# A fused attention and MLP kernel: a new order of its first stage, earlier fetches, masks built in one step, and another warm-up

## The chip, the cores and the metric

The kernel runs on one core of a Trainium2 chip. The core has engines that work side by side, each with its own queue of instructions taken in order: TensorE (PE: matmuls, and transposes done as matmuls), VectorE (DVE), ScalarE (ACT), GpSimd (POOL) and SyncE (SP, which here only issues DMAs). Inputs lie in the chip's main memory and come by DMA into on-chip memory (SBUF); TensorE writes its results into eight banks of PSUM. The metric is the device time of one execution in microseconds, shorter is better. Before the change three runs took 713.47, 714.91 and 716.59 us.

## The reference

Attention with four sink keys and a sliding window of 128 keys, over 4 batches, 8 heads, 768 positions and 64 dimensions; its output is the input of a two-layer MLP (512 to 2048 to 512) with a leaky ReLU.

```python
scores = scale * np.matmul(q, k.transpose(0, 1, 3, 2))
...
is_sink = pos[None, :] < int(n_sink)
rel = pos[:, None] - pos[None, :]
in_window = (rel >= 0) & (rel < int(window))
keep = is_sink | in_window
scores = np.where(keep, scores, -1000000000.0)
scores = scores - np.max(scores, axis=-1, keepdims=True)
a = np.exp(scores)
a = a / (np.sum(a, axis=-1, keepdims=True) + 1e-09)
attn_out = np.matmul(a, v)
x = attn_out.transpose(0, 2, 1, 3).reshape(B * S, H * D)
h = x @ w_in
g = np.maximum(0.01 * h, h)
out = (g @ w_out).astype(np.float32)
```

The two limits, sinks and window, are inputs, so the masks are made on the chip. The weights arrive as 64-bit numbers and are turned into 32-bit ones on the chip ("decoded").

## The kernel before

**Units.** The positions are cut into `NU` = 8 units of 384 rows (half a batch), a unit into `T` = 3 tiles of 128 queries. For each unit and head a tile's queries meet only the keys of their window: two blocks of 128 keys with the four sink keys between them (`W3` = 260 columns), or one block (128 columns) for the very first tile.

**Two forms of attention.** Units 0 and 1 (`EARLY` = 2) work on pairs of heads with plain 32-bit matmuls. Their tile goes through these steps: `scores_pair` (two score matmuls, one for each head, L283); `softmax_pair` (on DVE one instruction per head adds the mask and takes the row's extreme, L303; on ACT one exponential per head, which also sums its row, L305); `tail_pair`, called a turn below (two or four transposes on PE, L354 and L355, and a copy of them to SBUF on ACT, L357 or L360; POOL copies the sink columns, L358). After the third tile of a pair come `sinks` (one transpose, L386, a DVE product, L390, and a POOL copy of the sums, L395) and `values_pair` (value matmuls L412 and L414, three transposes L418, a copy on ACT, L419, the product on DVE, L421, and `emit_x`, which splits the result into a rounded part and the rest, L515 on ACT and L516 on DVE). Units 2 to 7 work head by head with rounded operands (fp32r) and are not touched.

**The MLP.** A unit's 384 rows go through 16 blocks of 128 hidden columns: twelve matmuls into bank `h` (L559), the leaky ReLU on ACT and DVE (L566, L567), a rounded part and the rest (L568, L569), and nine matmuls into three output banks (L580). Bank `h` is single: the next block may start when L567 has read the last one.

**Weights.** `load_weights` fetches one block of 512 KB, decodes it in three DVE steps (L172, L174, L176), rounds it on ACT (L180) and takes the rest on POOL (L181). `pace` ties the fetch to a softmax that lies `PRED` steps back in the stream, or, once four are decoded, to the decode of the fourth last.

**Order.** PE's order is written out by hand: two streams of steps (attention and MLP) are drawn in turn, and PE runs them as drawn. The other engines' orders are set by a scheduler that places each instruction among them. First the attention stream alone takes `early_steps + LEAD0` = 32 + 5 steps, which is unit 0 and part of unit 1 (called the first stage here). In it the softmax and scores of tile j are drawn, then what is pending: up to three steps, among them the turn of the tile before. Then the MLP of unit 0 begins, with the attention of unit 1 laced into it; from then on each unit's MLP runs beside a later unit's attention. SP issues its DMAs in order too: one that waits for a free buffer holds up those behind it.

**Start.** While the first loads run, PE does `WARM` = 22 matmuls on a tile of zeros (L604). `build_masks` makes three masks on DVE (first tile, m1, m2) from distances that POOL counts (L79, L81) and from the limits (L71 to L102); POOL then spreads m1 and m2 to the 260 columns that the early form needs (`wide`, L137 and L139).

Of the kernel before, what the change touches and what calls it, by code (L numbers as in the profile page):

```python
# [9 lines left out]
F32 = mybir.dt.float32  # L10
# [34 lines left out]
LEAD0 = 5  # L45
# [9 lines left out]
WARM = 22  # L55
DEPTH = 4
PRE0 = 5
PRED = 7
# [5 lines left out]
def build_masks(nc, cpool, tpool, lims):  # L64
    raw = tpool.tile([P, 2, 2], I32, name="lim_raw")
    words = lims.bitcast(I32).rearrange("(o w) -> o w", o=1)
    nc.sync.dma_start(out=raw.rearrange("p i w -> p (i w)"), in_=words.broadcast_to([P, 4]))
    lo = tpool.tile([P, 2], F32, name="lim_lo")
    hi = tpool.tile([P, 2], F32, name="lim_hi")
    lim = cpool.tile([P, 2], F32, name="lim")  # L70
    nc.vector.tensor_copy(out=lo, in_=raw[:, :, 0])  # L71
# [4 lines left out]

    rel = tpool.tile([P, 2 * P], F32, name="rel")
    key = tpool.tile([P, P], F32, name="key")
    nc.gpsimd.iota(rel, pattern=[[-1, 2 * P]], base=P, channel_multiplier=1,  # L79
                   allow_small_or_imprecise_dtypes=True)  # L80
    nc.gpsimd.iota(key, pattern=[[1, P]], base=0, channel_multiplier=0,  # L81
                   allow_small_or_imprecise_dtypes=True)
    cur = tpool.tile([P, P], F32, name="cur")
    prv = tpool.tile([P, P], F32, name="prv")
    m0 = cpool.tile([P, P], F32, name="m0")
    m1 = cpool.tile([P, WM], F32, name="m1")
    m2 = cpool.tile([P, WM], F32, name="m2")
    tri = cpool.tile([P, P], I8, name="tri")
    nc.vector.tensor_scalar(out=cur, in0=rel[:, P:], scalar1=0.0, scalar2=None, op0=ALU.is_ge)
    nc.vector.tensor_scalar(out=tri, in0=rel[:, P:], scalar1=0.0, scalar2=None, op0=ALU.is_lt)  # L90
    nc.vector.scalar_tensor_tensor(out=cur, in0=rel[:, P:], scalar=win, in1=cur, op0=ALU.is_lt, op1=ALU.mult)
    nc.vector.scalar_tensor_tensor(out=m0, in0=key, scalar=ns, in1=cur, op0=ALU.is_lt, op1=ALU.max)
    nc.vector.tensor_scalar(out=m0, in0=m0, scalar1=-1.0, scalar2=MASKED, op0=ALU.add, op1=ALU.mult)
    nc.vector.tensor_scalar(out=prv, in0=rel[:, 0:P], scalar1=win, scalar2=None, op0=ALU.is_lt)
# [13 lines left out]
    return lim, (m0, m1, m2), tri, diag  # L108
# [3 lines left out]
def fast_path(ctx, tc, cpool, qp, qk, vu, vs, w_in, w_out, out, ident, wz, lim, masks, tri, diag, negm, wmin, wmax):  # L112
# [20 lines left out]
    wide = []  # L133
    for n, m in enumerate(masks[1:]):
        e = apool.tile([P, W3], F32, tag="stg", name=f"wide{n}")
        for sign, base, dst in ((1, -1, e[:, 0:P]), (-1, 0, e[:, WM:])):
            nc.gpsimd.affine_select(out=dst, in_=m[:, NSK:], pattern=[[sign, P]], base=base,  # L137
                                    channel_multiplier=-sign, compare_op=ALU.is_ge, fill=-MASKED)
        nc.gpsimd.tensor_copy(out=e[:, P:WM], in_=m[:, 0:NSK])  # L139
        wide.append(e)  # L140
# [310 lines left out]
    def attend_pair(u, pair, pend, state):  # L451
# [12 lines left out]
        def gather():  # L464
            state["st"] = sinks(u, pair, sk, state)
# [361 lines left out]
```

## Time and profile before

| | before |
|---|---|
| runs shown, median (lowest to highest) | 714.91 us (713.47 to 716.59) |
| profiled execution: its time | 712.43 us |
| its span in the trace | 710.7 us |
| mean granted TensorE clock | 0.995 |
| bytes moved, share of DMA busy (queue 1) | 74.32 MB, 32.0% |

The table stands for the profiled execution except for its first row. The span runs from the first to the last instruction in the trace; 1.7 us lie around it. A row of the timeline has its start and its length in us, the engine (PEld is the loading of PE's stationary operand, SPq an issue of a DMA), the line, the operation and what it writes and reads, the shapes and a count where equal instructions follow one another; in brackets stands how long the engine had been idle, and what ended that. A row of the windows gives for a stretch of time its length and, for each engine, the time that it was busy.

### The profile page before, as it was taken

The numbers are of one execution on the slowest core, as the hardware profiler recorded it, in microseconds if no ns is written. First come the engines' busy times: TensorE is split into PE (matmuls) and PEld (weight loads), VectorE is DVE, ScalarE is ACT, GpSimd is POOL, SyncE is SP. The second block draws the span as 40 slices with busy tenths as digits, with TensorE's granted clock in tenths as the row PEclk, the third lists the DMA queues.
The fourth block names the chain that finished last, engine by engine and source line by source line (L and its number), as shares of the span: only waits on it lengthen the run. The fifth ranks groups of instructions, "written<-read, shape, count | busy, mean of one in ns | idle before, by whom it ended". The sixth has DMA issues, their size and how long they took to land.

```text
span 710.7 us, 12473 instructions
## 1 busy us (share of the span) xinstructions
PE 692.1 (97%) x3871; PEld 602.9 (85%) x3871; DVE 533.9 (75%) x1717; ACT 417.8 (59%) x1162; POOL 397.4 (56%) x536
## 2 busy tenths in 40 slices
PE   8799999999999999999999999999999999999995
PEld 4467778999899899998989799989899998999884
DVE  6788989666678888888889888888888978642222
ACT  5766666576656666666665676666667566422221
POOL 2346668555557777667666777748666665400000
PEclk9999999999999999999999999999999999999999
DMA  6756654221124342243324433334332310000001
GB/s 189 262 171 227 204 170 167 67 74 56 54 70 139 125 127 92 96 155 117 101 97 132 127 123 108 99 106 144 103 100 98 102 54 30 0 19 28 1 0 50
DMA packets 42603, 74.32 MB, mean 105 GB/s; under 512 B 3489, under 2 KB 26273, under 8 KB 42529
## 3 DMA queue, kind: packets, MB, share of 16 engines
q1 hardware_dynamic: 42384, 73.31, 32.0%
q8 instruction: 33, 0.54, 0.3%
q14 instruction: 42, 0.34, 0.2%
q10 hardware_dynamic: 144, 0.13, 0.1%
HBM read 67.14 MB, written 6.29 MB: 103 GB/s over the span
## 4 chain that ended last, share of the span: by engine, by line
PE 89%; DVE 5%; ACT 2%; DMA 1%; issue 1%; POOL 1%; POOLq 0%; ACTq 0%; DVEq 0%
PE h L559 36%; PE o L580 36%; PE v L439 5%; PE s L291 4%; PE t L365 2%; PE v L412 1%; PE s L283 1%; DMA wiraw<-in_w_in 1%; PE v L414 1%; DVE gl L569 1%; DMA woraw<-in_w_out 1%; PE t L386 0%; PE t L433 0%; PE t L355 0%; PE t L418 0%
## 5 line engine op out<-in xcount | busy, mean ns | idle before, releaser
L559 PE MATMUL h<-xh,wi 128*128 128x384 f32 x1024 | 311.3, 352 | 1.7 <-DVE g L567 1.3
L580 PE MATMUL o<-wo,gh 128*128 128x512 f32 x768 | 247.1, 403 | 0.0
L559 PEld LDWEIGHTS h<-xh,wi 128*128 128x128 f32 x1024 | 190.0, 188 | 16.7 <-issue 2.5
L559 PE MATMUL h<-xl,wi 128*128 128x384 f32 x512 | 172.8, 337 | 0.0
L335 POOL TENSOR_SCALAR_AFFINE_SELECT pt<-stg 128x256 fp32r<-128x256 f32 x240 | 105.3, 463 | 95.1 <-DVE stg L373 71.5
L580 PE MATMUL o<-wo,gl 128*128 128x512 f32 x384 | 151.4, 394 | 0.0
L580 PEld LDWEIGHTS o<-wo,gh 128*128 128x128 f32 x768 | 132.3, 189 | 17.2 <-issue 0.7
L567 DVE TENSOR_TENSOR g<-h,g 128x384 f32<-128x384 f32 x128 | 71.0, 555 | 64.0 <-ACT g L566 63.0
L566 ACT ACTIVATE g<-h 128x384 f32<-128x384 f32 x128 | 62.4, 487 | 70.1 <-PE h L559 68.8
L559 PEld LDWEIGHTS h<-xl,wi 128*128 128x128 f32 x512 | 96.9, 189 | 3.0
L580 PEld LDWEIGHTS o<-wo,gl 128*128 128x128 f32 x384 | 72.1, 188 | 17.9 <-DVE gl L569 0.2
L568 ACT CAST gh<-g 128x384 fp32r<-128x384 f32 x128 | 65.5, 511 | 35.1 <-DVE g L567 32.6
L569 DVE TENSOR_TENSOR gl<-g,gh 128x384 fp32r<-128x384 f32 x112 | 76.4, 682 | 11.5 <-ACT gh L568 9.9
L320 ACT ACTIVATE pk<-pk,negm 128x128 f32<-128x128 f32 (+1 forms) x144 | 58.1, 404 | 37.8 <-DVE negm L317 37.2
L242 POOL TENSOR_TENSOR qksp<-qkraw,qksp 64x392 fp32r<-64x392 f32 (+1 forms) x48 | 58.5, 1219 | 25.9 <-ACT qksp L241 18.0
L291 PEld LDWEIGHTS s<-qksp 128*128 128x128 f32 x288 | 53.2, 188 | 9.3 <-issue 2.9
L372 ACT CAST stg<-t 128x128 fp32r<-128x128 f32 x120 | 31.0, 258 | 47.9 <-PE t L365 34.0
L291 PE MATMUL s<-qksp 128*128 128x260 f32 (+1 forms) x288 | 56.3, 277 | 2.4 <-DVE negm L317 2.4
L244 POOL TENSOR_TENSOR qksp<-qkraw,qksp 128x384 fp32r<-128x384 f32 x48 | 51.9, 1082 | 3.8
L326 DVE TENSOR_SCALAR pk<-pk,sm 128x132 f32<-128x132 f32 (+1 forms) x120 | 47.5, 396 | 2.1
L439 PEld LDWEIGHTS v<-pt,vsp 128*128 128x128 f32 x336 | 45.1, 189 | 2.7 <-DVE xf L445 0.6
L241 ACT CAST qksp<-qkraw 128x776 fp32r<-128x776 f32 (+1 forms) x48 | 42.9, 893 | 6.7 <-PE s L291 3.4
(132 smaller groups left out, 1058.8 us busy)
## 6 DMA issues: line engine op xcount, KB each, us to landing
qkraw<-in_qk SPq DMA_DIRECT2D x24, 454.0 KB, 3.3
qkraw<-in_qk SPq DMA_DIRECT2D x24, 388.0 KB, 3.6
wiraw<-in_w_in SPq DMA_DIRECT2D x16, 512.0 KB, 3.8
woraw<-in_w_out SPq DMA_DIRECT2D x16, 512.0 KB, 3.8
ciraw<-in_w_in SPq DMA_DIRECT2D x16, 512.0 KB, 3.7
coraw<-in_w_out SPq DMA_DIRECT2D x16, 512.0 KB, 3.5
out<-ob SPq DMA_DIRECT2D x23, 256.0 KB, 2.0
vraw<-in_vu SPq DMA_DIRECT2D x14, 256.0 KB, 2.6
```

The lines of the kernel that those rows point to most:

```text
L242: nc.gpsimd.tensor_tensor(out=sp[D:P, TU:TU + n], in0=raw[D:P, TU:TU + n], in1=sp[D:P, TU:TU + n].bitcast(F32), op=ALU.subtract)
L244: nc.gpsimd.tensor_tensor(out=sp[:, TU + n:2 * TU + n], in0=raw[:, 0:TU], in1=sp[:, 0:TU].bitcast(F32), op=ALU.subtract)
L291: nc.tensor.matmul(ps[:, 0:kn], lhsT=sp[:, off + j * P:off + (j + 1) * P], rhs=sp[:, TU + k0:TU + k0 + kn], start=c == 0, stop=c == len(pa ...
L320: nc.scalar.activation(out=w, in_=w, func=AF.Exp, scale=-1.0, bias=neg, accum_out=sm)
L335: nc.gpsimd.affine_select(out=out, in_=src, pattern=([[0, x]] if x > 1 else []) + [[sign, P]], base=-1 if prev else 0, channel_multiplier= ...
L439: nc.tensor.matmul(out[:, o:o + m], lhsT=l, rhs=r, start=c == 0, stop=c == len(mms) - 1, skip_group_check=True)
L559: nc.tensor.matmul(ph[:, 0:TU], lhsT=w[:, cs], rhs=x, start=cc == 0 and c == 0, stop=cc == NCC - 1 and c == 2)
L566: nc.scalar.mul(g, ph[:, 0:TU], 0.01)
L567: anchor[0] = nc.vector.tensor_tensor(out=g, in0=ph[:, 0:TU], in1=g, op=ALU.max)
L568: nc.scalar.copy(out=gh, in_=g)
L569: (nc.gpsimd if u == 0 else nc.vector).tensor_tensor(out=gl, in0=g, in1=gh.bitcast(F32), op=ALU.subtract)
L580: nc.tensor.matmul(po[t], lhsT=gg[:, tsl], rhs=w, start=f == 0 and c == 0, stop=f == NFC - 1 and c == 2)
```

## The change

- **Order of units 0 and 1.** `attend_pair` goes; `early_stream` runs over all 24 tiles in one loop. A tile's scores and softmax are drawn `SAHEAD` = 2 tiles ahead of its turn. After the third turn of a pair the sinks are drawn at once, and the values after the scores of the next tile.
- **Fetches.** The values of pair 1 are loaded at the start, those of later pairs two ahead. A weight fetch is tied to a softmax 12 steps back (`PRED`; 7 before), while the distance between two weight loads stays 7 (`PERIOD`) and the first comes one step later (`PRE0` 6, was 5).
- **First stage.** It ends two steps sooner (`LEAD0` 3, was 5); the MLP of unit 0 begins there, and the two steps follow inside it.
- **Masks.** `build_masks` makes the two wide masks on DVE straight from the distances. The narrow ones are folded from them later (`fold_masks`). The setting of `diag` goes from DVE to POOL, and three checks of the limits go to the end (`check_limits`).
- **Warm-up.** 12 matmuls on the zeros as before, then 4 on a rounded tile of zeros (`st1`).
- **Last output tile.** Its two halves lie in two tiles instead of one.

```diff
-LEAD0 = 5
+LEAD0 = 3
+SAHEAD = 2
-WARM = 22
+WARM = 12
+WARMR = 4
-PRE0 = 5
-PRED = 7
+PRE0 = 6
+PERIOD = 7
+PRED = 12
...
+    nc.vector.scalar_tensor_tensor(out=keep, in0=rel, scalar=win, in1=keep, op0=ALU.is_lt, op1=ALU.mult)
+    nc.vector.scalar_tensor_tensor(out=m0, in0=key, scalar=ns, in1=keep[:, WM:], op0=ALU.is_lt, op1=ALU.max)
     nc.vector.tensor_scalar(out=m0, in0=m0, scalar1=-1.0, scalar2=MASKED, op0=ALU.add, op1=ALU.mult)
...
+    nc.vector.tensor_scalar(out=wide[0], in0=keep, scalar1=-1.0, scalar2=MASKED, op0=ALU.add, op1=ALU.mult)
+    nc.vector.tensor_scalar(out=keep[:, P:WM], in0=key[:, 0:NSK], scalar1=ns, scalar2=None, op0=ALU.is_lt)
+    nc.vector.tensor_scalar(out=wide[1], in0=keep, scalar1=-1.0, scalar2=MASKED, op0=ALU.add, op1=ALU.mult)
...
+def fold_masks(nc, cpool, wide):
+    folded = [cpool.tile([P, WM], F32, name=f"m{n + 1}") for n in range(2)]
+    nc.vector.tensor_tensor(out=folded[0][:, NSK:], in0=wide[1][:, 0:P], in1=wide[1][:, WM:], op=ALU.max)
+    nc.gpsimd.tensor_copy(out=folded[1][:, NSK:], in_=folded[0][:, NSK:])
+    for e, m in zip(wide, folded):
+        nc.gpsimd.tensor_copy(out=m[:, 0:NSK], in_=e[:, P:WM])
+    return folded
...
-        pace(dma, decoded[-DEPTH] if len(decoded) >= DEPTH else anchors[-PRED])
+        pace(dma, decoded[-DEPTH] if len(decoded) >= DEPTH else anchors[-min(PRED, len(anchors))])
...
+        for k, tile_ in enumerate(tiles):
+            score(*tile_)
+            yield
+            while pend:
                 pend.pop(0)[1]()
                 yield
...
+            if k >= SAHEAD:
+                u, pair, j = tiles[k - SAHEAD]
+                turn(u, pair, j)
+                yield
+                if j == T - 1:
+                    gather(u, pair)
+                    yield
+                    pend.append((1, lambda u=u, pair=pair: value(u, pair)))
...
+                            nc.scalar.copy(out=obs[0], in_=po[t][:, 0:256])
+                            nc.scalar.dma_start(out=out[r0:r0 + P, 0:256], in_=obs[0])
+                            nc.vector.tensor_copy(out=obs[1], in_=po[t][:, 256:])
+                            nc.sync.dma_start(out=out[r0:r0 + P, 256:], in_=obs[1])
...
+    for _ in range(WARMR):
+        nc.tensor.matmul(warm[:, 0:TU], lhsT=sts[1][:, 0:P], rhs=sts[1], start=True, stop=True)
```

Three places show what this does to the engines' orders. In the names `s0_4_2` are the scores of unit 0, head 4, tile 2; `t` a transpose's bank, `pe0_2_1` the exponentials of unit 0, pair 2, tile 1; the last number only tells buffers apart.

PE before, from the scores of unit 0's pair 2 (heads 4 and 5), tile 2, to that tile's turn:

```order
L283 MATMUL s0_4_2_406<-qkp0_2_192 128x260
L283 MATMUL s0_5_2_407<-qkp0_2_192 128x260
L354 MATMUL t12_416<-ident_60,pe0_2_1_353 128x128
L355 MATMUL t12_416<-ident_60,pe0_2_1_353 128x128
L354 MATMUL t12_416<-ident_60,pe0_2_1_353 128x128
L355 MATMUL t12_416<-ident_60,pe0_2_1_353 128x128
L283 MATMUL s0_6_0_429<-qkn0_3_241 128x128
L283 MATMUL s0_7_0_430<-qkn0_3_241 128x128
L354 MATMUL t13_437<-ident_60,pe0_2_2_405 128x128
L355 MATMUL t13_437<-ident_60,pe0_2_2_405 128x128
```

PE of the changed kernel, first what follows the same scores, then where the same tile's turn stands:

```order
L284 MATMUL s0_4_2_340<-qkp0_2_167 128x260
L284 MATMUL s0_5_2_341<-qkp0_2_167 128x260
L413 MATMUL v0_1_350<-pt0_1_209,vn0_1_163 64x256 x4
L413 MATMUL v0_1_350<-pt0_1_209,vn0_1_163 64x128 x2
L415 MATMUL v0_1_350<-sn0_1_335,vsraw0_1_164 128x256
L419 MATMUL t10_358<-ident_60,rs1_337 128x128 x3
L356 MATMUL t11_373<-ident_60,pe0_2_0_291 128x128 x2
```

```order
L284 MATMUL s0_6_1_409<-qkn0_3_205 128x260
L284 MATMUL s0_7_1_410<-qkn0_3_205 128x260
L355 MATMUL t13_417<-ident_60,pe0_2_2_339 128x128
L356 MATMUL t13_417<-ident_60,pe0_2_2_339 128x128
L355 MATMUL t13_417<-ident_60,pe0_2_2_339 128x128
L356 MATMUL t13_417<-ident_60,pe0_2_2_339 128x128
L387 MATMUL t14_424<-ident_60,sk0_2_288 16x128
```

Between a tile's scores and its turn stood one turn and one pair of scores; now the values of a pair, a short turn (pair 2, tile 0), the scores of tile 0 of pair 3, the turn of tile 1 and the scores of tile 1 of pair 3 stand there.

DVE before, from the limits to the first softmax:

```order
L91 SCALAR_TENSOR_TENSOR cur_84<-rel_80,lim_75,cur_84 128x128
L94 TENSOR_SCALAR prv_85<-rel_80,lim_75 128x128
L99 TENSOR_SCALAR m2_88<-key_81,lim_75 128x4
L631 TENSOR_SCALAR bad_8872<-lim_75 128x1
L632 TENSOR_SCALAR bad_8872<-lim_75 128x1
L633 TENSOR_SCALAR bad_8872<-lim_75 128x1
L92 SCALAR_TENSOR_TENSOR m0_86<-key_81,lim_75,cur_84 128x128
L95 TENSOR_TENSOR m1_87<-cur_84,prv_85 128x128
L96 SCALAR_TENSOR_TENSOR m1_87<-key_81,lim_75,prv_85 128x4
L101 TENSOR_SCALAR m2_88<-m2_88 128x4
L93 TENSOR_SCALAR m0_86<-m0_86 128x128
L98 TENSOR_SCALAR m1_87<-m1_87 128x132
```

(then the two casts of `st` and a copy, L130 and L102). DVE of the changed kernel, the same stretch whole, with the first softmax:

```order
L93 SCALAR_TENSOR_TENSOR keep_111<-rel_109,lim_108,keep_111 128x260
L94 SCALAR_TENSOR_TENSOR m0_115<-key_110,lim_108,keep_111 128x128
L96 SCALAR_TENSOR_TENSOR keep_111<-key_110,lim_108,keep_111 128x4
L95 TENSOR_SCALAR m0_115<-m0_115 128x128
L98 TENSOR_SCALAR wide0_117<-keep_111 128x260
L99 TENSOR_SCALAR keep_111<-key_110,lim_108 128x4
L100 TENSOR_SCALAR wide1_118<-keep_111 128x260
L111 TENSOR_TENSOR m1_565<-wide1_118 128x128
L304 ISA pe0_0_0_172,negm_65<-s0_0_0_173,m0_115 128x128
```

Fifteen instructions behind the limits become eight; the casts of `st` now stand ahead of the limits, and the fold of the narrow mask (L111) was drawn up to just before the first softmax.

SP before, from its sixth DMA:

```order
L204 DMA qkp0_2_192<-in_qp0 128x776
L223 DMA vn0_1_219<-in_vu0 128x384
L223 DMA vsraw0_1_220<-in_vs 128x128
L204 DMA qkn0_3_241<-in_qp0 128x776
L152 DMA wiraw0_315<-in_w_in 128x4x256
L223 DMA vraw0_2_300<-in_vu0 128x384
L223 DMA vsraw0_2_301<-in_vs 128x128
L204 DMA qkn1_0_332<-in_qp1 128x908
L153 DMA woraw0_391<-in_w_out 128x1024
```

SP of the changed kernel, from the same place:

```order
L224 DMA vn0_1_163<-in_vu0 128x384
L224 DMA vsraw0_1_164<-in_vs 128x128
L205 DMA qkp0_2_167<-in_qp0 128x776
L153 DMA wiraw0_300<-in_w_in 128x4x256
L205 DMA qkn0_3_205<-in_qp0 128x776
L154 DMA woraw0_377<-in_w_out 128x1024
L205 DMA qkn1_0_286<-in_qp1 128x908
L224 DMA vraw0_2_278<-in_vu0 128x384
L224 DMA vsraw0_2_279<-in_vs 128x128
```

The first two weight blocks move ahead of loads that wait for buffers: `wiraw0` ahead of the queries and keys of pair 3, `woraw0` ahead of those of unit 1's first pair and of the values of pair 2.

More of the change, by code (lines that the diff above doesn't have):

```diff
@@ L75, in build_masks @@
     ns, win = lim[:, 0:1], lim[:, 1:2]
[L77 to L85, printed above, removed]
@@ L107, in build_masks, with fast_path @@
                                 channel_multiplier=sign, compare_op=ALU.is_ge, fill=0.0)
-    return lim, (m0, m1, m2), tri, diag
+    return lim, m0, wide, tri, diag
+def fold_masks(nc, cpool, wide):
[5 more added lines that the diff above has]
+    return folded
 @with_exitstack
-def fast_path(ctx, tc, cpool, qp, qk, vu, vs, w_in, w_out, out, ident, wz, lim, masks, tri, diag, negm, wmin, wmax):
+def fast_path(ctx, tc, cpool, qp, qk, vu, vs, w_in, w_out, out, ident, wz, lims, negm, wmin, wmax):
     nc = tc.nc
@@ L131, in fast_path @@
         sts.append(st)
[L133 to L140, printed above, removed]
+    lim, m0, wide, tri, diag = build_masks(nc, cpool, mpool, iopool, apool, lims)
+    masks = [m0]
     xs = [[] for _ in range(NU)]
@@ L482, in attend_late @@
+        pend.append((0, lambda: gather(u, pair)))
+        pend.append((1, lambda: value(u, pair)))
     def attend_late(u, h, pend, state):
@@ L526, in attention_stream @@
         load_values(0, 0)
-        for u in range(EARLY):
-            for pair in range(NPAIR):
-                yield from attend_pair(u, pair, pend, state[pair % 2])
+        load_values(0, 1)
+        yield from early_stream(pend)
         for u in range(EARLY, NU):
@@ L624, in fast_path, with check_limits @@
             next(stream, None)
-    return flags[0]
-def needs_general(nc, pool, row, ident, lim, negm, wmin, wmax):
+    return flags[0], lim
+def check_limits(nc, pool, lim):
     bad = pool.tile([P, 6], F32, name="bad")
-    deep = pool.tile([P, 1], F32, name="deep")
     nc.vector.tensor_scalar(out=bad[:, 0:1], in0=lim[:, 0:1], scalar1=float(NSK), scalar2=None, op0=ALU.is_gt)
@@ L633, in needs_general @@
     nc.vector.tensor_scalar(out=bad[:, 2:3], in0=lim[:, 1:2], scalar1=float(P), scalar2=None, op0=ALU.is_gt)
+    return bad
+def needs_general(nc, pool, row, ident, bad, negm, wmin, wmax):
+    deep = pool.tile([P, 1], F32, name="deep")
     nc.vector.tensor_reduce(out=deep, in_=negm, axis=AX.X, op=ALU.max)
```

115 lines of the change are left out of this document (58 added, 57 removed).

## The prediction

> **What bounds the kernel now.** I read the busy times first, then the slices, then windows, then TensorE's own waits.
>
> ```profile
> PE 692.1 (97%) x3871; PEld 602.9 (85%) x3871; DVE 533.9 (75%) x1717; ACT 417.8 (59%) x1162; POOL 397.4 (56%) x536
> ...
> PE   8799999999999999999999999999999999999995
> ...
> PE s L291 <- DVE negm L317: 2.4, 2, 1.5
> PE h L559 <- DVE g L567: 1.3, 1, 1.3
> ...
> 6.30:41.20 34.90, 28.76 (x181) 15.87 (x181) 25.00 (x94) 24.78 (x81) 9.79 (x24) 0.95 0.65 211
> 60.00:80.00 20.00, 20.00 (x115) 15.51 (x114) 18.09 (x40) 11.91 (x30) 11.66 (x13) 1.00 0.60 200
> ```
>
> TensorE is the bound: 97% busy, and in the 40 slices only the first three and the last fall short. The waits are those of TensorE from 46 to 700 us: 2.4 us before late scores, 1.3 in starting unit 0's second hidden block. The change leaves the later work alone, so whatever it gains lies in the first 46 us and at the very end. The columns of a window are TensorE, weight load, VectorE, ScalarE, GpSimd, granted clock, DMA share. From 6.3 to 41.2 us, the first stage, TensorE is busy 28.8 of 34.9 us, and VectorE and ScalarE are not far behind, 25.0 and 24.8. Removing TensorE's waits there is worth what these two let it have.
>
> Its waits in the stage, from the timeline of TensorE (start, length, in brackets the idle time before):
>
> ```profile
> 7.78 0.67 PE L355 MATMUL t<-ident,pe 128*128 128x128 f32 x2 [0.59 <-POOL wide L139]
> ...
> 16.81 0.33 PE L354 MATMUL t<-ident,pe 128*128 128x128 f32 x1 [0.41 <-ACT pe L305]
> ...
> 17.78 0.33 PE L354 MATMUL t<-ident,pe 128*128 128x128 f32 x1 [0.54 <-ACT pe L305]
> ...
> 25.03 0.33 PE L354 MATMUL t<-ident,pe 128*128 128x128 f32 x1 [1.65 <-ACT pe L305]
> ...
> 33.33 0.33 PE L354 MATMUL t<-ident,pe 128*128 128x128 f32 x1 [2.10 <-ACT pe L305]
> ...
> 34.34 0.33 PE L354 MATMUL t<-ident,pe 128*128 128x128 f32 x1 [0.58 <-ACT pe L305]
> ...
> 45.71 0.45 PE L559 MATMUL h<-xh,wi 128*128 128x384 f32 x1 [1.31 <-DVE g L567]
> ```
>
> Six waits of turns make 5.87 us; nearly all are for exponentials. The two long ones come from behind ScalarE, as VectorE and SP show:
>
> ```profile
> 20.78 0.69 DVE L172 TENSOR_SCALAR do<-woraw 128x512 int32<-128x512 int32 x1 [0.49 <-DMA woraw<-in_w_out]
> ...
> 29.86 0.69 DVE L172 TENSOR_SCALAR di<-wiraw 128x512 int32<-128x512 int32 x1 [2.00 <-DMA wiraw<-in_w_in]
> ...
> 24.12 0.38 SPq L152 DMA_DIRECT2D wiraw<-in_w_in  x1
> ```
>
> VectorE stood 2.00 us in front of a decode whose fetch was issued at 24.12 and landed at about 29.8, and the softmax behind it in VectorE's queue stood too. And the long wait is followed by slow matmuls:
>
> ```profile
> 26.75 1.30 PE L412 MATMUL v<-pt,vraw 128*64 128x256 f32 x12
> ...
> 29.30 0.71 PE L283 MATMUL s<-qkn 64*128 64x260 f32 x4
> ...
> 34.71 1.23 PE L283 MATMUL s<-qkn 64*128 64x260 f32 x4
> ...
> 36.18 2.27 PE L412 MATMUL v<-pt,vn 128*64 128x256 f32 x12
> ...
> 36.50:37.50 1.00, 1.00 (x6) 0.47 (x4) 0.50 0.00 0
> ```
>
> The same scores take 1.23 instead of 0.71 us, the same values 2.27 instead of 1.30, and the granted clock there (the last row, a window of L412 alone) is 0.50. That costs 0.52 + 0.97 = 1.5 us.
>
> The Trainium skill, "TensorE: Matmul & The Clock Gate", section "Part 1: The HAM clock gate", says the clock halves after at least one idle window of about 3.4 us. By that rule no wait here is long enough, and the sum below would be 1.5 us less; the trace does not bear it out so far.
>
> The slow stretch begins 1.2 us after the end of the 2.10 us wait, with the 0.58 us one between, and TensorE's clock is granted in full elsewhere between 6 and 46 us, so I let the waits own it.
>
> **The start.**
>
> ```profile
> 1.26 0.89 SPq L204 DMA_DIRECT2D qkn<-in_qp  x2
> ...
> qkn<-in_qp SPq DMA_DIRECT2D x1, 388.0 KB, 4.0
> ...
> 1.19 5.13 PE L604 MATMUL warm<-wz 128*128 128x384 bf16 x22 [1.19 <-DVE wz L770]
> ...
> 4.04 1.89 PEld L604 LDWEIGHTS <-wz 128*128 128x128 bf16 x12 [0.17 <-issue]
> 6.25 0.52 PEld L283 LDWEIGHTS s<-qkn 64*128 64x128 f32 x8 [0.32 <-issue]
> ...
> 4.53 0.35 DVE L91 SCALAR_TENSOR_TENSOR cur<-rel,lim,cur 128x128 f32<-128x128 f32 x1
> 4.80 0.28 DVE L94 TENSOR_SCALAR prv<-rel,lim 128x128 f32<-128x128 f32 x1
> ...
> 6.85 0.29 DVE L303 CUSTOM_DVE_ANT_0 pe<-s,m 128x128 f32<-128x128 f32 x1
> 7.06 0.09 DVE L303 DVE_READ_ACCUMULATOR2_ANT negm<- 128x1 f32 x1
> ...
> 7.52 0.43 DVE L303 CUSTOM_DVE_ANT_0 pe<-s,wide 128x260 f32<-128x260 f32 x1 [0.16 <-POOL wide L139]
> 7.87 0.08 DVE L303 DVE_READ_ACCUMULATOR2_ANT negm<- 128x1 f32 x1
> ```
>
> The first queries and keys, issued at 1.26, took 4.0 us and so lay there at 5.26 us, but the warm-up ran to about 6.2. Ten of its 22 weight loads come before 4.04; the other twelve follow at 1.89/12 = 0.16 us. Twelve matmuls end near 4.5; the four rounded ones, of the same 384 columns and also taken at 0.16, near 5.2 (their tile is cast ahead of the limits now). The first scores then wait for the data, 5.4 instead of 6.25: **0.85 us**. If a rounded matmul takes twice that, they start at 5.8.
>
> The masks. From the limits (4.53) eight instructions lead to the first softmax. One of 128 columns holds VectorE 0.27 us (4.53 to 4.80); L303 shows that 260 instead of 128 columns add 0.14 (0.35 against 0.21, start to start). So L93 0.40, L94 0.27, L95, L96 and L99 about 0.13 each, L98 and L100 about 0.21, the fold L111 0.20, and some 0.2 for results waited for: 6.4 us instead of 6.85. The wide masks lie there at once, so the second softmax comes at 6.85 instead of 7.52. The POOL work on them and the three checks hide; the copies of the fold are in POOL's slack (9.8 of 34.9 us busy).
>
> **The first stage.** No work of TensorE goes: two turns and scores of unit 1, some 1.2 us, move behind the second hidden block, and I compare at equal work. A pair needs, without waits, this much of TensorE:
>
> ```profile
> 21.36 0.38 PE L355 MATMUL t<-ident,pe 128*128 128x128 f32 x2
> ...
> 28.98 0.38 PE L355 MATMUL t<-ident,pe 128*128 128x128 f32 x2
> ...
> 9.69 0.51 ACT L305 ACTIVATE pe<-pe,negm 128x260 f32<-128x260 f32 x1 [0.34 <-DVE negm L303]
> ...
> 10.20 0.50 ACT L305 ACTIVATE pe<-pe,negm 128x260 f32<-128x260 f32 x1
> ```
>
> From one first turn of a pair to the next, 7.62 us less the wait of 1.65: 6.0 us. From a tile's scores to its turn lay one turn and one pair of scores, about 1.1 us; softmax and two exponentials (0.35 + 2 x 0.51) cannot be done in that. Now a whole value step, two turns and two pairs of scores lie between, over 4 us. So the waits for exponentials go, unless the queues of VectorE or ScalarE are behind. Those carry, for each pair and one weight block, 25.0 and 24.8 us over some 4.5 pairs, 5.5 us each: under 6.0, but close.
>
> The fetches. A weight fetch is now tied to a softmax five steps earlier, over 4 us at 0.9 us a step. The second input block would be issued near 16 and land near 22 us even at the 5.7 us of before, in front of a decode that stands near 26; the first two pass the loads that wait for buffers in SP's queue. Pair 2's queries and keys go behind pair 1's values (0.9 us later) and are needed only near 14 us. So both DMA waits go, with the 2.00 us the long turn waits and the slow stretch.
>
> What is late next is ScalarE. Walking its new order: the first turn still waits 0.3 us; the values of pair 0 wait 0.4, for the copy of the third tile queues behind exponentials; and in each of pairs 1 to 3 something like 0.45 goes, where a turn's PSUM bank waits for the copy of the sums (L419 before) or the values for the last copy. That is 2.1 us of new waits. Its ends are 0, since both engines have less work than TensorE, and 4.9, if each of four pairs loses the 0.95 that pair 1 lost before (rows 16.81 and 17.78) and the start about 1 more (two exponentials). I take 2.1, which the walk gives; it is nearer to the row of 0.95 for one pair than to four of them.
>
> The 1.31 us before the second hidden block stays: nothing stands between the two blocks on TensorE, and the bank is single. If VectorE is late with the decode ahead of it, it grows to 1.7.
>
> **The end.**
>
> ```profile
> 703.97 0.42 DVE L590 COPY ob<-o 128x256 f32<-128x256 f32 x1 [0.41 <-ACT ob L588]
> ```
>
> With two tiles VectorE need not wait 0.41 us for ScalarE's half. SP's issues may be the later limit, so between 0 and 0.4; I take 0.2.
>
> **The sum.** 0.85 + 5.87 - 2.1 + 1.5 + 0.2 = **6.3 us**. Against the profiled execution, 712.43 us (a span of 710.7 and 1.7 around it), that is 706.1; this execution lies 2.5 us under the median of the runs, 714.91, which gives **708.6 us**, 0.9% less.
>
> **The rivals.**
> *All waits hide* (new waits 0.3, the end 0.4, half the block wait gone): 0.85 + 5.87 - 0.3 + 1.5 + 0.4 + 0.6 = 8.9 us, 706.0. For it: both other engines have less to do than TensorE; against it: by only half a microsecond a pair, in fixed queues. Chance 0.17.
> *ScalarE or VectorE sets the pace*, new waits at their upper end and the clock falls once more: 0.85 + 5.87 - 4.9 + 0.2 = 2.0 us, 712.9. The loads near 5.5 of 6.0 speak for it. Chance 0.14.
> *The slow stretch isn't owed to the waits* and stays, at whatever place: 6.3 - 1.5 = 4.8 us, 710.1. For it: the wait of 1.65 us at 25.03 left no such stretch behind it; against it: the longest did. Chance 0.07. (This is the case of the skill's rule above.)
> *The fetches aren't early*, because SP still stands behind a load that waits for its buffer: the 2.10 us wait and the slow clock stay, 6.3 - 3.6 = 2.7 us, 712.2. Against it: the first two blocks stand ahead of such loads. Chance 0.06.
> *Slower: VectorE falls behind in unit 0's MLP.*
>
> ```profile
> 50.67 0.55 DVE L567 TENSOR_TENSOR g<-h,g 128x384 f32<-128x384 f32 x1
> ...
> 51.30 0.43 PE L559 MATMUL h<-xh,wi 128*128 128x384 f32 x1
> ```
>
> L567 ended at 51.22 and the next hidden block, which needs its bank, began at 51.30: a reserve of 0.08 us, with VectorE 90% busy (60 to 80 us). If the shorter first stage leaves VectorE one decode step (0.69 us) later in each of the 16 blocks, TensorE loses 16 x 0.69 = 11 us: 4.7 us slower, 719.6. It decides for a loss once more than nine blocks lose a step. Against it: VectorE's order around a block is nearly the same, and TensorE gets 1.2 us more to do there. Chance 0.06.
>
> **How the numbers follow.** My forecast has 0.50. About 0.5% (3.6 us) is what a measurement of this kernel can tell from no change. Faster by more: the forecast, whose own spread of 4 to 8 us lies above that, and the first and third rivals, with a little off for small sizes and a little from the second: 0.74. Within: the second and fourth, 0.20. Slower: 0.06. The range goes from the first rival less 2 us for the scatter of the runs, 704.0, to the second and a little more, 713.3; the slower case is left out.
>
> **What would show it.** The first score at 5.4 us; the first softmax near 6.4; no decode waiting for a DMA before 46 us; granted clock 1.00 throughout; TensorE's waits in the first stage 2 us instead of 5.9, for ScalarE's copies and not for exponentials; the first hidden block near 33.8 us (41.2 before) and the second near 38.2 (45.71). It is wrong if turns still wait over a microsecond for exponentials, if a matmul of the stage runs at half speed, or if waits for L567 appear in unit 0's MLP.

## The result, and the profile after

| | before | after |
|---|---|---|
| median (lowest to highest) | 714.19 us, 6 runs (712.27 to 716.59) | 709.40 us, 6 runs (708.34 to 710.35) |
| profiled execution, its span | 712.43 us, 710.7 us | 710.29 us, 708.5 us |
| first hidden block starts | 41.20 us | 33.70 us |
| second hidden block starts | 45.71 us | 38.67 us |
| outputs of unit 0 issued from | 138.32 us | 135.08 us |
| last matmul starts | 703.13 us | 700.10 us |

The ratio of the medians is 0.9928, 95% interval 0.9907 to 0.9948: 4.8 us less, where 6.3 us were forecast. The two profiled executions differ by only 2.1 us. That gap is the main thing to explain, beside the terms of the sum.

The page of the changed kernel, its busy times:

```profile
PE 691.5 (98%) x3865; PEld 603.2 (85%) x3865; DVE 535.2 (76%) x1714; ACT 416.7 (59%) x1162; POOL 396.6 (56%) x535
```

The waits of its TensorE from 46 to 700 us, in all, times, longest:

```profile
PE s L292 <- DVE negm L318: 2.4, 2, 1.5
PE o L599 <- POOL gl L588: 0.8, 1, 0.8
```

The 2.4 us stood there before too; the 0.8 us is new, and a wait of 0.3 us behind VectorE is gone.

The windows of the first stage of before, and of 20 to 40 us, in the changed kernel (columns as in the prediction; the granted clock is the third from the end):

```profile
6.30:41.20 34.90, 30.57 (x197) 18.20 (x194) 30.08 (x103) 27.93 (x89) 12.02 (x23) 0.97 0.76 253
...
20.00:40.00 20.00, 16.88 (x107) 10.67 (x105) 19.54 (x56) 16.17 (x48) 8.38 (x13) 0.98 0.80 269
```

TensorE is busier in the stage (30.6 us of 34.9, was 28.8), and so are VectorE (30.1, was 25.0) and ScalarE (27.9, was 24.8); VectorE has no slack left from 20 to 40 us, 19.5 of 20. (TensorE's 30.6 us include a stretch at half clock, below.) The clock is 0.97 on average: the slow clock has not gone. TensorE's timeline of the changed kernel, its waits up to 46 us and the first row of the first hidden block:

```profile
7.17 0.91 PE L284 MATMUL s<-qkn 64*128 64x260 f32 x4 [0.31 <-DVE negm L304]
11.66 0.27 PE L387 MATMUL t<-ident,sk 128*16 128x128 f32 x1 [0.89 <-POOL rs L396]
21.74 0.33 PE L355 MATMUL t<-ident,pe 128*128 128x128 f32 x1 [0.37 <-ACT rs L420]
23.99 0.27 PE L387 MATMUL t<-ident,sk 128*16 128x128 f32 x1 [0.37 <-ACT pt L358]
30.50 0.27 PE L387 MATMUL t<-ident,sk 128*16 128x128 f32 x1 [0.41 <-ACT pt L358]
33.70 0.42 PE L578 MATMUL h<-xh,wi 128*128 128x384 f32 x1
...
36.88 0.44 PE L578 MATMUL h<-xl,wi 128*128 128x384 f32 x1 [0.72 <-DVE xl L536]
38.67 0.45 PE L578 MATMUL h<-xh,wi 128*128 128x384 f32 x1 [1.18 <-DVE g L586]
```

The six waits of turns are gone. In their place stand five of 2.35 us together (0.31 + 0.89 + 0.37 + 0.37 + 0.41), and two before hidden blocks, 0.72 and 1.18 us. No decode of VectorE waits for a DMA before 46 us. The wait for `xl` is not only a matter of order. VectorE's and GpSimd's timelines of the changed kernel at that place, then VectorE's of e11 (below), where nothing runs on GpSimd meanwhile:

```profile
35.70 1.13 DVE L536 TENSOR_TENSOR xl<-xf,xh 128x384 fp32r<-128x384 f32 x1
...
35.13 1.28 POOL L182 TENSOR_TENSOR wo<-wof,wo 128x512 fp32r<-128x512 f32 x1 [1.47 <-DMA qkn<-in_qp]
```

```profile
37.20 0.54 DVE L536 TENSOR_TENSOR xl<-xf,xh 128x384 fp32r<-128x384 f32 x1
```

The same instruction takes twice as long beside GpSimd's rest: 1.13 us with 0.71 us of overlap, 0.54 with none. So up to 0.6 of the 0.72 us can be that overlap; no run took it away by itself. Right behind the last two waits the clock falls. The same part in windows of 3.41 us:

```profile
35.96:39.38 3.42, 1.52 (x7) 1.00 (x7) 3.35 (x6) 2.11 (x4) 0.95 (x2) 1.00 0.43 148
39.38:42.79 3.41, 3.41 (x12) 2.31 (x11) 2.43 (x7) 1.26 (x4) 3.06 (x3) 0.50 0.75 226
```

For 3.41 us TensorE runs at half clock and does half of the work: 1.7 us lost. And at the end of the changed kernel VectorE's last copy now waits for a DMA (timeline):

```profile
703.02 0.42 DVE L609 COPY ob_io<-o 128x256 f32<-128x256 f32 x1 [2.50 <-DMA out<-ob]
```

The second half of the last tile lies in an `io` tile, of which there are two, and both still hold tiles on their way out. The span ends 8.4 us after the start of the last matmul, 0.8 us more than before (7.6).

The runs of after fall into two groups: 708.3 to 708.7 us (mean clock 0.997 to 0.998) and 710.1 to 710.4 us (0.995 to 0.996), three each. The profiled one is of the second. The mean clock is only a coarse sign of slow stretches, since it also counts the half clock that TensorE has after its last work (from 705.0 us in this profile): 0.996 stands for one slow stretch in e3's profile below and for none in e9's.

### The profile page after: what moved, and what is told of

The parts are those of the page before. It is cut to its first block, busy times and chain, and to the rows that moved or that the text cites. A ratio compares the mean times of both kernels' runs of the same rounds, so it can differ in the third digit from the quotient of the medians.

```text
span 708.5 us, 12445 instructions
## 1 busy us (share of the span) xinstructions
PE 691.5 (98%) x3865; PEld 603.2 (85%) x3865; DVE 535.2 (76%) x1714; ACT 416.7 (59%) x1162; POOL 396.6 (56%) x535
## 4 chain that ended last, share of the span: by engine, by line
PE 83%; DVE 10%; ACT 2%; DMA 2%; issue 1%; POOL 1%; DVEq 0%; ACTq 0%; POOLq 0%
PE h L578 34%; PE o L599 34%; PE v L440 5%; PE s L292 4%; PE t L366 2%; PE s L284 1%; PE v L413 1%; DVE pe L304 1%; DVE di L173 1%; DVE g L586 1%; DVE di L175 1%; DVE wif L177 1%; DVE gl L588 1%; DVE do L175 1%; DMA qkn<-in_qp 0%
## 5 line engine op out<-in xcount | busy, mean ns | idle before, releaser
L310 DVE COPY_PREDICATED s<-tri,s 128x128 f32<-128x128 int8 x120 | 34.7, 289 | 17.1 <-PE s L292 16.1
```

## The experiments

Each was compared with the kernel before on the same chip. Medians in us:

| run | against | median (runs) | ratio to before, 95% |
|---|---|---|---|
| e1 | after | 709.98 (6) | 0.9934, 0.9911 to 0.9957 |
| e2 | after | 711.36 (12) | 0.9957, 0.9944 to 0.9970 |
| e3 | before | 712.21 (12) | 0.9973, 0.9959 to 0.9987 |
| e4 | before | 711.16 (10) | 0.9957, 0.9940 to 0.9974 |
| e5 | after | 706.54 (4) | 0.9896, 0.9879 to 0.9913 |
| e6 | after | 709.21 (6) | 0.9941, 0.9926 to 0.9955 |
| e7 | after | 709.10 (6) | 0.9935, 0.9921 to 0.9949 |
| e9 | e5 again | 707.41 (6) | 0.9906, 0.9885 to 0.9927 |
| e10 | e9 | 705.58 (5) | 0.9878, 0.9855 to 0.9902 |
| e11 | e10 | 707.63 (6) | 0.9910, 0.9888 to 0.9933 |
| e12 | e11 | 707.12 (6) | 0.9902, 0.9881 to 0.9923 |

### Order alone, fetches alone (e3, e4)

Before with the new order (e3: `early_stream` and the early value loads as in the diff of the change, with these numbers), and before with the new fetch times (e4):

```diff
-LEAD0 = 5
+LEAD0 = 3
+SAHEAD = 2
```

```diff
-PRE0 = 5
-PRED = 7
+PRE0 = 6
+PERIOD = 7
+PRED = 12
```

> The kernel before with the new order of units 0 and 1, the earlier value loads and the shorter first stage alone; weight fetches tied as before (7 steps back), masks, warm-up and end as before. Theory (order and fetches need each other): TensorE's waits for exponentials go, but VectorE stands in front of decodes for their fetches, 3 us or more in all, and the gain is 1.5 to 3 us, 711.2 to 712.7. Rival (the order does it alone): no wait of VectorE for a fetch above 1 us, a gain of 4 to 5 us, 709.2 to 710.2.

> The kernel before with the earlier weight fetches alone (12 steps back, first load one step later); order, masks, warm-up and end as before. Theory: VectorE's waits of 2.00 and 0.49 us for fetches go, and with them the 2.10 us wait of TensorE and the slow clock behind it; the 0.4 to 1.7 us waits for exponentials stay; a gain of 2 to 3.6 us, 710.6 to 712.2. Rival (the exponentials take the place of the fetch): under 1 us, 713.2 or more.

Waits of e3 from 6 to 46 us, VectorE's for decodes, then two of TensorE's:

```profile
DVE do L173 <- DMA woraw<-in_w_out: 2.1, 1, 2.1
...
DVE di L173 <- DMA wiraw<-in_w_in: 0.4, 1, 0.4
...
PE h L578 <- ACT xh L535: 1.1, 1, 1.1
...
PE h L578 <- DVE xl L536: 0.5, 1, 0.5
```

With the order alone TensorE waits for exponentials no more, and its longest wait in the stage is 0.89 us. But VectorE still stands 2.5 us before decodes, and TensorE waits for ScalarE's and VectorE's parts of the first hidden block's operands; that the one brings the other is argued, not shown. TensorE's timeline of e4, whose VectorE waits for no DMA:

```profile
24.48 0.33 PE L355 MATMUL t<-ident,pe 128*128 128x128 f32 x1 [0.42 <-ACT pe L306]
25.45 0.33 PE L355 MATMUL t<-ident,pe 128*128 128x128 f32 x1 [0.54 <-ACT pe L306]
32.22 0.33 PE L355 MATMUL t<-ident,pe 128*128 128x128 f32 x1 [0.95 <-ACT pe L306]
...
43.03 0.45 PE L560 MATMUL h<-xh,wi 128*128 128x384 f32 x1 [1.32 <-DVE g L568]
```

The fetches alone take the two long waits away (1.65 to 0.42 us, 2.10 to 0.95 us), and the second hidden block comes 2.7 us earlier. So either change takes the two long waits away, and only the order takes the short ones.

The two gains in the medians, 2.5 and 3.6 us, make more than the 4.8 us of the whole change, so they are no split of it. Much of them is clock. e4's runs have a mean of 0.996 to 0.998, and its profile has no slow stretch between 6 and 700 us; of its 2.7 us at the second hidden block 1.7 are the slow stretch that before had. Against before's ten runs of the higher clock (near 712.8 us, next section) e4 gains 1.6 us, what one slow stretch costs. e3's profile has one slow stretch, as before's has, and its last matmul starts 0.6 us sooner (702.51 against 703.13). By this estimate at like clock, order and fetches bring under a microsecond each alone, and 2.6 together with the rest of the change: they need each other, as the theory of e3 said.

### The clock (e8, e5, e9, e2)

Seventeen of the 27 runs of before beside e1 to e4 lay between 713.9 and 716.8 us with a mean clock of 0.989 to 0.992, ten at 712.2 to 713.4 us with 0.994 to 0.996. The first profile, 712.43 us at 0.995, is like the ten. A second profile of the unchanged kernel:

> The kernel before, unchanged, for a second profile. Its 27 runs here fall in two clusters, ten near 712.8 us with a mean granted clock of 0.994 to 0.996 and seventeen near 715.2 with 0.989 to 0.992, and the profile at hand is of the first. Theory: the upper cluster has a second stretch of half clock (3.4 us long, about 1.7 us lost) that the changed kernel never has, so about half of the 4.8 us between the medians is clock. If this profile falls in the upper cluster, a second window with granted clock 0.50 is seen somewhere in the first 60 us; rival: the clock is lower evenly, or elsewhere in the span.

It took 716.38 us with a mean clock of 0.990. Windows of 3.41 us, first of the first profile of before, then of this one:

```profile
31.35:34.76 3.41, 0.85 (x6) 0.45 (x6) 3.29 (x12) 2.98 (x10) 0.90 (x1) 1.00 0.61 201
34.76:38.18 3.42, 3.42 (x18) 1.76 (x17) 2.70 (x9) 2.09 (x8) 1.39 (x5) 0.50 0.27 95
```

```profile
24.10:27.51 3.41, 1.46 (x11) 0.72 (x9) 3.21 (x13) 2.91 (x10) 1.46 (x2) 1.00 0.91 282
27.51:30.92 3.41, 3.41 (x16) 1.75 (x17) 1.14 (x6) 1.94 (x7) 0.70 (x2) 0.50 0.79 258
30.92:34.33 3.41, 3.41 (x25) 1.91 (x21) 2.76 (x6) 1.53 (x4) 0.00 (x0) 1.00 0.81 230
34.33:37.75 3.42, 2.16 (x15) 1.13 (x15) 3.08 (x13) 3.19 (x11) 2.04 (x4) 1.00 0.87 260
37.75:41.16 3.41, 3.41 (x18) 1.94 (x13) 2.58 (x8) 1.10 (x4) 0.24 (x2) 0.50 0.21 59
41.16:44.57 3.41, 3.41 (x15) 2.42 (x15) 1.72 (x6) 2.52 (x7) 1.27 (x1) 0.50 0.74 234
```

Three slow windows instead of one, at other places, though the program is the same. Their edges lie on one grid of 3.41 us (27.51 to 37.75 is three steps). In before's first profile the same grid, counted back from 34.76, passes 4.04 us, just where its warm-up turned fast. The clock is decided step by step on a grid that does not start with the program; its place differs from run to run. The Trainium skill, "TensorE: Matmul & The Clock Gate", section "Part 1: The HAM clock gate", says that the window is 3.413 us long and runs free; these traces agree. It speaks of an idle window; here windows with TensorE 0.85 to 2.16 us busy were followed by a slow one. (That 41.16 stayed slow after a window full of work is not explained by this.)

So a wait does not own a slow stretch: what counts is whether the idle time that lies close together falls into one step of the grid. In after, 0.72 + 1.18 us lie within 2.5 us; the step that was shown with the result (35.96 to 39.38) caught both. e6 (below) has the same two waits, 0.78 and 1.18 us, but in its profile an edge of the grid falls at 36.78 us, inside the first of them; its windows:

```profile
36.78:40.19 3.41, 2.07 (x10) 1.51 (x12) 3.24 (x7) 1.52 (x3) 1.25 (x2) 1.00 0.49 159
40.19:43.60 3.41, 3.41 (x20) 2.76 (x19) 3.35 (x9) 2.49 (x8) 2.44 (x4) 1.00 0.77 255
```

No slow step follows. To test it from the other side, e5 and again e9 draw two more steps of attention ahead of the first hidden block, so that `xl` is ready:

```diff
-LEAD0 = 3
+LEAD0 = 5
```

> The changed kernel with LEAD0 = 5 instead of 3: the first pair of scores of unit 1's second pair stands ahead of the first hidden block again, so the rest xl of pair 3 is ready when the block asks for it. Theory (the slow stretch behind the first hidden block is owed to the waits of 0.72 us for xl and 1.18 us for the bank, which fall close together): the 0.72 us wait shrinks below 0.2, the slow stretch near 39.5 us is gone from the profile, most runs lie in the upper cluster of mean clock (0.997 or more), and the median falls to about 708.4 us. Rival (the stretch comes by chance at a place of its own, whatever the waits): the wait goes but a stretch of about 3.4 us at half clock is still seen in half of the runs, and the median stays within 0.5 us of the changed kernel's 709.4 to 710.

> The kernel of e5 again (the changed kernel with LEAD0 = 5), as the ground for the next three, since its runs lay within a microsecond of each other. Theory of the clock (decided anew every 3.41 us on a grid that runs free of the kernel; a stretch of the grid in which TensorE is busy for less than about two thirds is followed by one at half clock): no wait of this kernel leaves over 1.2 us idle in any 3.41 us but the 1.18 us one by itself, so no run has a slow stretch: mean clock 0.996 or more in all of them and all within about 706.4 to 707.4 us. Rival (e5 was lucky): some runs near 708.2 with a mean clock of 0.995.

TensorE's timeline of e5, where the first hidden block begins and its next wait:

```profile
35.03 0.44 PE L578 MATMUL h<-xh,wi 128*128 128x384 f32 x1
...
39.14 0.45 PE L578 MATMUL h<-xh,wi 128*128 128x384 f32 x1 [1.18 <-DVE g L586]
```

The wait for `xl` is gone, and the granted clock is 1.00 in every window from 5 to 60 us. All ten timed runs of e5 and e9 lie between 706.4 and 708.1 us (707.4 at most was expected of e9), without the two groups of after; no run has the rival's 0.995. In the clock the theory held.

The gain is larger than the 709.4 to 708.4 us that were expected, and not all of it is clock. On the same chip the runs of e6 and e7, which keep the two waits, lie at 708.4 to 710.7 us, e5's at 706.4 to 707.3. The profiles of e7 and e5 have no slow step, and still e5's last matmul starts 1.8 us sooner (696.83 against 698.59): the wait of 0.7 us for `xl` is gone, and so is the one of 0.8 us for POOL's rest (`gl`) that after and e7 have later, at which e5 was not aimed. The slow step comes on top in part of after's runs. Against before the ratios are 0.9928 for after, 0.9896 and 0.9906 for e5 and e9; these intervals overlap.

The limit of two thirds in e9's theory does not hold. Nor is 1.18 us the longest wait of that kernel: at 395.8 us TensorE waits 1.53 us before late scores, as in every kernel here near 400 us. Windows of before there, on its grid:

```profile
399.99:403.40 3.41, 1.88 (x12) 1.55 (x11) 3.18 (x8) 1.11 (x5) 1.96 (x3) 1.00 0.79 247
403.40:406.82 3.42, 3.33 (x18) 2.67 (x17) 3.35 (x12) 2.29 (x8) 2.95 (x4) 1.00 0.14 52
```

Only 1.88 of 3.41 us are busy, and the clock stays at 1.00. So it is in all fourteen profiles, twelve of them with 1.88 to 1.90 us busy in that step, the other two with 2.06 and 2.12.

The old warm-up in after (22 plain matmuls) kept the two waits:

```diff
-WARM = 12
-WARMR = 4
+WARM = 22
+WARMR = 0
```

> The changed kernel with the warm-up of before: 22 matmuls on zeros, none rounded. Theory (the warm-up only decides when the first scores start, and masks hold the first softmax anyway): first scores at about 6.3 instead of 5.92, first softmax unchanged near 6.8, time the same within 0.4 us, 709.4 to 709.8. Rival (the shorter warm-up is worth what the forecast gave the start): 0.8 us slower, 710.2.

All twelve runs lay at 710.8 to 712.7 us with a mean clock of 0.994 to 0.996. The median is 2.0 us above after's, more than theory (0.4) and rival (0.8) had allowed. The first scores start at 6.45 us, and the second hidden block came only 0.17 us later than in after, the last matmul 0.4 us; after it the span runs on for 8.9 us (8.4 in after). Its windows show the same picture:

```profile
35.18:38.59 3.41, 1.76 (x10) 1.15 (x9) 3.38 (x6) 1.87 (x5) 1.28 (x1) 1.00 0.67 224
38.59:42.00 3.41, 3.16 (x10) 2.29 (x10) 2.18 (x4) 1.41 (x3) 2.61 (x3) 0.50 0.53 165
```

Why, by the mean clock, the step caught the waits in all of these runs and in half of after's stays open, and so does the rest of the 2.0 us.

### The start (e6, e7)

The fold of the masks moved behind the first stage; and after without the four rounded warm-up matmuls:

```diff
-WARMR = 4
+WARMR = 0
...
-    masks.extend(fold_masks(nc, cpool, wide))
+    with tc.issue_after(anchor[0].ins):
+        masks.extend(fold_masks(nc, cpool, wide))
```

> The changed kernel with the fold of the narrow masks tied to the last softmax of the first stage instead of drawn in front of the first softmax. Theory (the first stage starts when VectorE is done with the masks, and the fold stands in that chain): the first softmax comes at about 6.6 instead of 6.82 us, everything behind it in the stage moves up by 0.2, and the first hidden block starts near 33.5 instead of 33.7; the time falls by about 0.2 us, less than the runs can show. Rival (the stage is paced by ScalarE, so the start does not matter): first softmax earlier, first hidden block unchanged at 33.7.

> The changed kernel without the four rounded warm-up matmuls (12 plain ones only). Theory (the start is bound by the masks on VectorE, not by TensorE): the first scores come at about 5.3 us, when their data lie there, instead of 5.92, but the first softmax stays at 6.8 and the rest of the stage with it, so the time stays within 0.3 us at equal clock. Rival (the scores bind the start): the first softmax moves up by 0.4 us or more and the time falls by as much. A third possibility: TensorE idles for 0.5 us, its clock is released later, and the first turns take up to twice as long, 1 to 2 us slower.

The timeline of after, with the rounded warm-up and the first scores on TensorE, the fold and the first softmax on VectorE:

```profile
4.75 1.24 PE L628 MATMUL warm<-st 128*128 128x384 f32 x4
5.92 0.93 PE L284 MATMUL s<-qkn 64*128 64x128 f32 x8
...
6.61 0.29 DVE L111 TENSOR_TENSOR m<-wide 128x128 f32<-128x128 f32 x1
6.82 0.28 DVE L304 CUSTOM_DVE_ANT_0 pe<-s,m 128x128 f32<-128x128 f32 x1
```

In the timeline of e6 the same, without the fold, then in that of e7 the first scores and the first softmax:

```profile
4.75 1.60 PE L628 MATMUL warm<-st 128*128 128x384 f32 x4
6.29 1.79 PE L284 MATMUL s<-qkn 64*128 64x128 f32 x12
...
6.81 0.29 DVE L304 CUSTOM_DVE_ANT_0 pe<-s,m 128x128 f32<-128x128 f32 x1 [0.23 <-PE s L284]
```

```profile
5.14 1.29 PE L284 MATMUL s<-qkn 64*128 64x128 f32 x8
...
6.40 0.28 DVE L304 CUSTOM_DVE_ANT_0 pe<-s,m 128x128 f32<-128x128 f32 x1
```

Without the fold VectorE waits 0.23 us for the scores, and the softmax comes no sooner. But in this run the scores themselves are late: the four rounded matmuls took 1.60 us instead of 1.24, as a clock that rose later would give, and the scores start 0.37 us later than in after. So e6 does not decide between its theory and its rival. In after the first softmax follows the fold with no wait, so masks and fold come last there. In e7 the scores come 0.8 us earlier; there the schedule also put the fold behind the first two softmaxes, and the first softmax comes at 6.40, right behind the masks (the last begins at 6.19), the first hidden block at 33.31 instead of 33.70. That is the size that its rival gave, but the fold's new place explains it without the scores; the run does not separate the two. Both medians are within the scatter of after's runs.

### The end (e1, e10)

The second half of the last tile in a tile of another tag, `g`, that is free by then; e1 does it in after, e10 in e9:

```diff
-                            obs = [iopool.tile([P, 256], F32, tag=tag, name=f"ob{v}_{tag}", bufs=n)
-                                   for tag, n in (("wraw", 1), ("io", None))]
+                            obs = [iopool.tile([P, 256], F32, tag="wraw", name=f"ob{v}_wraw", bufs=1),
+                                   mpool.tile([P, TU], F32, tag="g", name=f"ob{v}_g")[:, 0:256]]
```

> The changed kernel, with the second half of the last output tile in a buffer that has long been free (a tile of the hidden activations) instead of one of the two output buffers. Theory (the output buffer is still being sent): the 2.50 us wait of VectorE before its last copy goes, the copy follows the last matmul at once, and the end of the span comes about 7 us after the last matmul instead of 8.0; 0.8 to 1.7 us less than the changed kernel, about 708.4. Rival (the last DMA is limited by SP's issue before it, or by the work behind it): the wait goes but the time stays at 709.4.

> The kernel of e9 with the second half of the last output tile in a buffer that is free by then (tag g). Theory: the 2.2 to 2.5 us that VectorE waits at the end for a DMA is shortened to 0.4 us, the last DMA is issued some 1.6 us sooner, and the time falls by about 0.85 us, to about 705.7. Rival (the end is set by the two DMAs in front in SP's queue): the wait goes but the time stays within 0.3 us of e9.

The timeline of e10, VectorE's last copy:

```profile
697.54 0.42 DVE L609 COPY ob_g<-o 128x256 f32<-128x256 f32 x1 [0.41 <-ACT ob_wraw L607]
```

The wait for the DMA is gone, but not the 0.41 us for ScalarE's half: with two SBUF tiles the two copies from one PSUM bank still run one after the other. In e1 the span ends 7.7 us after the start of the last matmul instead of 8.4, but in the times the gain is lost in the two groups of runs (five of six lie at 709.6 to 710.4 us). In e10, free of them, the median falls by 1.8 us against e9 on the same chip, and no run of e10 is as slow as the fastest of e9 (706.15 against 706.76). The two profiled spans, 705.6 and 704.4 us with the last matmul at the same time, show 1.2 us of it; another 0.4 us lies outside the spans (706.15 less 704.4 against 707.75 less 705.6). e10 is the best version of this study: 1.2% under before.

### More of the start, and the gap between the hidden blocks (e11, e12)

e11 is e10 with the edits of e6 and e7 together; e12 adds to it that the first turn and scores of unit 1 in the MLP are drawn between the first two hidden blocks:

```diff
-            due = early_steps + LEAD0 + (early_steps + LEAD - LEAD0) * (x + 1) // mlp_steps
+            due = early_steps + LEAD0 + (early_steps + LEAD - LEAD0) * x // mlp_steps
+            if x >= NCC - 1:
+                due = max(due, early_steps + LEAD0 + 2)
```

> The kernel of e10 without the four rounded warm-up matmuls and with the fold behind the first stage. Theory (masks and scores both bind the first softmax, so only both edits together move the start): first softmax at 6.4 us and the third at 6.8 (7.24 and later before), first hidden block 0.4 to 0.6 us earlier than in e10, time about 0.5 us lower, 705.2. Rival (ScalarE's exponentials set the pace by then): first hidden block less than 0.2 us earlier.

> The kernel of e11 with the first turn and the next scores of unit 1 drawn between the first and the second hidden block instead of inside them. Theory (the 1.18 us before the second block is TensorE waiting for the leaky ReLU of the first, with nothing else drawn between): the 0.5 us turn and the 0.65 us scores run in that time, the wait shrinks to 0.1 to 0.3 us, and the time falls by 0.5 to 1 us, to about 704.4. Rival (VectorE, which decodes weights there without a pause, falls behind instead): the wait goes but one for decoded weights or for VectorE comes behind it, and the time stays.

The first softmax of e11 came as expected at 6.43 us (as in e7, so e11 does not show that both edits are needed), the first hidden block at 34.68 us (35.00 in e10), between theory and rival. But the time rose, to 707.63 us where 705.2 was expected: the fold now stands on VectorE ahead of `xl` and takes 1.19 us there (0.29 in after), beside GpSimd's rest again, and the wait that e5 had removed is back. TensorE's timeline of e11:

```profile
37.79 0.44 PE L578 MATMUL h<-xl,wi 128*128 128x384 f32 x1 [0.67 <-DVE xl L536]
39.58 0.52 PE L578 MATMUL h<-xh,wi 128*128 128x384 f32 x1 [1.18 <-DVE g L586]
```

Its windows of 3.41 us:

```profile
36.38:39.80 3.42, 1.58 (x9) 1.00 (x8) 3.38 (x7) 1.96 (x6) 0.57 (x4) 1.00 0.17 69
39.80:43.21 3.41, 3.41 (x11) 2.31 (x11) 2.02 (x4) 0.95 (x2) 3.07 (x3) 0.50 0.68 178
```

With it come the two groups: three runs at 706.8 to 707.1 us, three at 708.1 to 709.1 (clock 0.994 to 0.995). This was not meant, and is the clearest test of the clock: the pair of waits back, the slow step back in the profile and, by the mean clock, in half of the runs. In e12 the 1.18 us wait is filled, but `xl` is waited for longer (its timeline):

```profile
37.79 0.44 PE L578 MATMUL h<-xl,wi 128*128 128x384 f32 x1 [1.08 <-DVE xl L536]
```

The clock stays up (0.997 to 0.999 in its runs), which fits one wait by itself, but the time, 707.12 us, is above e10's and far from the 704.4 us expected: the case of the rival, VectorE falling behind. The gain of the filled gap could not be told apart from the cost of the fold.

## Why the prediction was right, and where not

The time came near the forecast (709.4 against 708.6 us), but in good part by luck: of the 4.8 us the profiled executions show 2.1, and the rest is clock, which the forecast had taken as fixed between its profile and the median. By its steps, in the profiled executions:

- **Waits for exponentials, 5.87 us; new waits, 2.1.** Right in the main. The six waits of turns (one of them for a mask) are gone and 2.35 us of new ones stand in the stage. Three of the five, 1.15 us, are behind ScalarE's copies as forecast; the longest, 0.89 us, is behind POOL's copy of the sums. The range of 0 to 4.9 was wide.
- **"No decode waiting for a DMA", fetches early.** Right; and e3 and e4 show that order and fetches need each other.
- **The step missed: what the first hidden block waits for.** With `LEAD0` 3 nothing stands between the last values of unit 0 and the block, and VectorE makes `xl` too late: 0.72 us. I had walked ScalarE's new order, not VectorE's, for the block's own operands, and had not seen that `xl` runs beside GpSimd's rest. The later wait of 0.8 us for POOL's rest was not foreseen either (0.5 us more than the 0.3 that went).
- **"So I let the waits own it", 1.5 us of slow clock gone.** This step failed. The runs fit idle time gathered in one step of a free grid. The 2.10 us wait was one such place, and the 0.72 + 1.18 us made another: one step of 3.41 us at half clock before and one after, so plus 1.5 became nothing in the profiled execution. (The two rows that gave 1.5 covered most of the step; the whole is 1.7.) In half of after's runs the step went, by their mean clock. The rival in which the stretch stays "at whatever place" was right for the others, at a chance of 0.07; that its 4.8 us is also the fall of the medians is chance.
- **The start, 0.85 us.** First scores 5.92 us, not 5.4: in this profile the twelve plain matmuls were taken at 0.32 us each to the end, where before's went on at 0.16 from 4.04 us, and the rounded took 0.31. First softmax 6.82, not 6.4: the fold was counted, but the masks' instructions were sized too small (start to start L93 0.60 us for 0.40, L98 and L100 0.33 for 0.21, L99 0.27 for 0.13). About 0.3 us came of it (first softmax with a wide mask 7.24 us, 7.52 before).
- **Second hidden block, 1.31 us stays.** Right: 1.18.
- **The end, plus 0.2.** Wrong in sign: about 0.8 lost. I looked at the wait that two tiles remove and not at which buffers the new tile comes from.

Together: 0.3 + 5.87 - 2.35 - 0.72 + 0.13 - 0.5 - 0.8 = 1.9 us of the 2.2 between the spans (710.7 less 708.5); 0.3 us is left without a term.

What made 4.8 us of it in the medians is, as far as the runs show, the clock again. I took it that the 2.5 us between before's profiled execution and its median stay. e8 has three slow steps instead of one, and the mean clocks of before's runs suggest that most have more than one; that its longer waits are the reason is argued. The change removed those too. At like clock (before's ten runs near 712.8, after's three near 710.2) the gain is 2.6 us.

The rival on the slower side was not seen: between 46 and 700 us TensorE waits for no hidden bank.

## What to carry to other kernels

Before counting on a clock that falls behind a wait, add up TensorE's idle time over any 3.41 us, and compare several runs' mean clocks: short waits close together can cost more through the clock than they last. The sum is a warning and no rule, as the windows near 400 us show. Take a second profile of a kernel before comparing terms of a microsecond. When a stage is cut shorter, look at what the next stage's first instruction waits for on every engine. When one tile becomes two, look at the pool that the second comes from, and who still holds its buffers.

## What was not expected of the hardware

The granted clock of the same program differs between runs by the place of a grid of 3.41 us: one slow step in one profile of before and three in another, and a warm-up that turned fast at 4.04 us in the first and near 7 us in the second. Steps of the grid between 6 and 46 us with TensorE busy for 1.76 us or less were followed by half clock in every profile; one with 2.16 us was too (e8), others with 2.07 (e6) and 2.09 us (e4) were not, and the steps near 400 us with 1.88 us were not either. What e5 has at the least in any 3.41 us around its 1.18 us wait is 2.22 us, and no run of e5, e9 or e10 shows a slow step by its mean clock; in e10's profile a step of the grid has 2.23 us there, and none follows. The window of e5:

```profile
35.80:39.20 3.40, 2.22 (x15) 1.75 (x13) 3.37 (x8) 2.73 (x9) 1.43 (x2) 1.00 0.47 160
```

So the busy time of the records alone does not give the limit. The steps near 400 us hold matmuls on rounded operands, those of the first stage mostly plain 32-bit ones; whether that is the difference was not tried.

VectorE's `xl` (1.13 us for 0.54) and the fold (1.19 for 0.29) took far longer when they began while GpSimd was at its own two-operand instruction of 1.3 us. And two engines copied the halves of one PSUM bank one after the other (0.41 us) with separate SBUF tiles too; whether the bank or the order between the instructions does that was not tried.
